# Linear attention with gates and a feed-forward layer: four masks of the first step go from VectorE to ScalarE and GpSimd, and the first step's matmuls are put in another order

## The chip, the cores and the metric

The kernel runs on one core of one Trainium2 chip. The metric is the device time of one execution in microseconds (us). The kernel before took 467.71, 467.12 and 467.70 us in three runs, a median of 467.7 us. A change of under 0.2% (0.94 us) is about what a measurement of this kernel cannot tell from no change.

## The reference, cut to what matters

Four batches, eight heads, 768 tokens, head size 48. A gated linear attention is followed by a feed-forward layer of 384 to 2048 to 384 with a piecewise activation:

```
f = 1 / (1 + exp(-f_logit))
for t in range(S):
    state = f[:, :, t, :, None] * state + einsum('bhd,bhde->...', k[:, :, t], v[:, :, t])
    y[:, :, t] = einsum('bhd,bhde->bhe', q[:, :, t], state)
x = y.transpose(0, 2, 1, 3).reshape(B * S, H * D)          # 3072 x 384
h = x @ w_in                                               # 384 -> 2048
g = where(h >= 1, h, where(h <= -1, 0, (h + 1) ** 2 / 4))
out = g @ w_out                                            # 2048 -> 384
```

## The kernel before, in words

**Tiles and stages.** The tokens are taken in six steps of 128 (C) for all four batches (B), so 512 columns (N) at a time. Within a step the recurrence is written as matrix products: scores (keys times queries, each scaled by running products of the gates), a mask that keeps the pairs with an earlier key, and the masked scores times the values. The feed-forward layer takes each step's 512 columns in 16 units of 128 hidden rows: nine 128x512 matmuls into `ph` (L317; unit 0 is written out at L960), the activation on ScalarE and VectorE (L320 to L334), and nine into `po` (L341). Its products are made of high and low halves, which is why there are nine. 96 units in all fill most of the time.

**The start.** Before unit 0 can begin, step 0's attention has to be ready. Its gates come in three tiles, 0 to 2; a fourth pair of heads rides in spare rows of the three ("last"). For each tile VectorE runs a scan into `w` (L546), a reciprocal (L552), a second scan (L553), and multiplies keys (L556) and queries (L558) in `kq`; tiles 0 and 2 are taken in two halves of 256 columns. TensorE then makes the scores of a tile (L638, into two PSUM banks), and the scores of the last pair (L668), whose keys ScalarE has copied to `kn` (L662). VectorE multiplies each bank by the 0/1 mask, which is a constant in `fixed` (L681, `masks`): `am` 0 to 3 for the banks of tiles 0 and 1, and `act`, `kn`, `am` 0 and 1 again for tile 2 and the last pair. TensorE multiplies the masked scores by the values: two groups "first" (L917, `heads`) that need the masks of tiles 0 and 1, then four groups "second" (L932, `thirds`, and L917) that need the others. The results are rounded to `x` (L761 on ScalarE, L762 on VectorE), and unit 0 starts.

**GpSimd** (POOL) has small work only: three instructions of 2 to 4 columns for each gate tile (L550, L563, L565).

**What sets the order.** Every operation is recorded with an engine, a cost in ns (`COST`) and what it needs. `Plan.order` plays them through by these costs and emits each engine's instructions in the order that comes out; `LOOK` names the engines that may pass over a ready operation for a more urgent one that is nearly ready. TensorE's operations keep the order in which they were recorded, which the tuple `START` gives for step 0. Where the plan foresees TensorE idle, it puts fillers in, matmuls on a tile of zeros into a bank that nobody reads (L396, `warm`); how many is worked out in `zeros_for`:

```
if o.start < 20000 and gap > 250:
    return int(gap / (330 if o.start < 10000 else 230)) + 1
return int(gap * 0.9 / 230) if gap > 500 else 0
```

A filler is emitted into TensorE's own stream and keeps its place there like any other matmul; what TensorE really waits for at run time does not change their number.

Of the kernel before, what the change touches and what calls it, by code (L numbers as in the profile page):

```python
# [19 lines left out]
ALU = mybir.AluOpType  # L20
PSUM = bass.MemoryType.PSUM

B, H, S, D = 4, 8, 768, 48
C = 128
# [28 lines left out]
LATENCY = dict(PE=235, ACT=140, DVE=110, POOL=150)  # L53
COST = dict(mm=227, narrow=120, scores=1000, scores_half=500, heads=960, thirds=1020, half=330, both=940, begin=430, before=880, part=450, states=700, before_half=440, parts=730, parts_last=730, zeros=4000, turn=395, first=160, last=200,
            rows=316, turned_rows=150, scan=1140, dve=602, small=200, sums=467, gate=600, act=575, bits=660, round=485, copy=520, turned=412, sig=538, decay=226,
            issue=480, near=600, least=300)


INSTRUCTIONS = dict(scores=32, scores_half=16, heads=32, thirds=32, both=128, begin=64, before=128, before_half=64, part=64, states=64, parts=128, parts_last=64, zeros=24, turn=8)
BLOCK, FIRST_BLOCK, AHEAD, BEHIND, FETCH, OFFSET, WAITS = 256, 193, 48, 40, 3700, 9, 1.0045  # L60


LOOK, MARGIN, GAP = ("ACT", "DVE"), 100, 3000

SOONER = 2000
GATHER_BEHIND, GATHER_LATER = (0, 0, 0), 6000
# [2 lines left out]
VISITS = {4: (8.0, 8.0, 11.0, 11.0), 6: (11.0, 12.5, 12.5, 12.5), 8: (21.0, 21.0, 22.0, 22.0), 10: (25.0, 25.0, 28.5, 28.5), 12: (28.5, 34, 36.0, 36.0), 14: (36.0, 42.5, 42.5, 42.5), 16: (49.0, 49.0, 55.0, 55.0), 18: (54.0, 55.0, 57.0, 57.0), 20: (66.0, 66.0, 75.0, 75.0), 22: (75.0, 77, 77, 77)}  # L69
HOMES = [(k + 3) % 5 for k in range(25)]  # L70
START = (("scores", 0), ("mask", 0, 0), ("mask", 0, 1), ("last", 0), ("scores", 1), ("mask", 1, 0), ("mask", 1, 1), ("last", 1),
         ("scores", 2, 0), ("last", 2, 0), ("scores", 2, 1), ("last", 2, 1), ("first", 0), ("first", 1),
         ("mask", 2, 1), ("mask", 3, 1), ("mask", 2, 0), ("mask", 3, 0), ("second", 0), ("second", 1), ("second", 2), ("second", 3))
AFTER = {1: (('turn', 0), ('turn', 1), ('turn', 2)), 4.5: (('states', 0), ('states', 2)), 2: (('turn', 3),)}

# [23 lines left out]
class Plan:  # L99
# [7 lines left out]
    def add(self, engine, cost, emit, *deps, kb=0, count=None):  # L107
        flat, made = [], count is not None

        def spread(d):  # L110
            if isinstance(d, list):
                for e in d:
                    spread(e)
            elif d is not None and d not in flat:
                flat.append(d)

        spread(list(deps))
        cost, kind = COST[cost] if isinstance(cost, str) else cost, cost
        count = count or INSTRUCTIONS.get(kind) or 2 * max(1, round(cost / (COST["mm"] if cost % COST["mm"] == 0 else COST["narrow"])))
        if engine == "PE":  # L120
            if self.tensor is not None and self.tensor not in flat:
                flat.append(self.tensor)
            small = made or kind in SMALL_PRODUCTS
            cost += (COST["last"] if small else COST["first"]) if small != self.small else 0
            self.small = small
        o = Op(engine, cost, emit, flat, kb)
        if engine == "PE":
            o.count = count
        for d in flat:
            d.users.append(o)  # L130
        if engine == "PE":
            self.tensor = o
        self.ops.append(o)
        return o
# [96 lines left out]
def gla_moe(ctx: ExitStack, tc: tile.TileContext, ff, kqd, f0, vv, vad, vbd, wd, fixedd, gates, values, headsd, out):  # L231
    nc = tc.nc
# [4 lines left out]
    def tiles(count, shape, dtype, name):  # L237
        return [const.tile(shape, dtype, name=f"{name}_{k}") for k in range(count)]
# [11 lines left out]
    am = tiles(4, [C, B, C], F32, "am")  # L250
# [28 lines left out]
    def wide(a):  # L279
        return a.rearrange("r b c -> r (b c)")  # L280

    def part(t, k):

        return t[:, k * N:(k + 1) * N].rearrange("r (b c) -> r b c", b=B)

    def whole(t):
        return t[:, 2 * N:]
# [63 lines left out]
    add = plan.add  # L351

    def dma(dst, src, kb, *deps):
        return add("SP", "issue", lambda: nc.sync.dma_start(dst, src), *deps, kb=kb)
# [4 lines left out]
    def vec(cost, fn, *deps):  # L359
        return add("DVE", cost, fn, *deps)  # L360

    def sca(cost, fn, *deps):
        return add("ACT", cost, fn, *deps)
# [130 lines left out]
    banks = {k: [] for k in range(8)}  # L494
# [11 lines left out]
    gates_of = [None] * (NI * NT)  # L506
# [3 lines left out]
    def old(n, *names, of=att):  # L510

        return [] if n < 0 else [of[n].get(k) for k in names]

    def gate(m):

        i, p = divmod(m, NT)
        t = kq[p]

        ft, before = (f[m], None) if m < 2 else (act_f[1], None) if m == 2 else (f[(m - 1) % 2], m - 3 if m < 5 else m - 2)
        et = end[m % 2]  # L520
        steps = ((0, 2), (2, 4)) if m in (0, 2) else ((0, 4),)
        count = len(steps)
        c = gates_of[m] = {k: [] for k in ("km", "qm", "sg", "en", "s1", "s2")}
        lk = c["lk"] = dma(t[:, 0:2 * N], kqd[i, p], 512, old(NP * (i - 1) + p, "sc", "y", "tr"),
                           old(m - NT, "km", "qm", "to", of=gates_of))
        if m == 0:
            ready["mask"] = ready["mask_t"] = ready["ident"] = dma(fixed, fixedd, 160)
            ready["f0"] = sca(200, lambda: nc.scalar.activation(f0s[:, 0:NI * NT * B], f0s[:, 0:NI * NT * B], AF.Sigmoid), dma(f0s, f0, 36))
        for h, (b0, b1) in enumerate(steps):
            cols = slice(b0 * C + (1 if b0 else 0), b1 * C + 1)  # L530
            if m != 2:
                l = dma(ft[:, cols], ff[i, p, :, cols], 256 // count, gates_of[before]["qm"] if before is not None else None)
            elif h == 0:
                l = dma(ft[:, 0:N + 1], ff[i, p, :, 0:N + 1], 256)
                l.early = SOONER
            last = old(m - 1, "km", "en", "s2", of=gates_of)
            u0, u1 = B - b1, B - b0
            fwd = ft[:, b0 * C:b1 * C]
            bwd = ft[:, b1 * C:b0 * C:-1]
            kt, qt = wide(part(t, 0)[:, u0:u1]), wide(part(t, 1)[:, b0:b1])  # L540
            if m != 2:
                sg = sca("sig" if count == 1 else 308, lambda cols=cols: nc.scalar.activation(ft[:, cols], ft[:, cols], AF.Sigmoid), l)  # L542
            elif h == 0:
                sg = sca("sig", lambda: nc.scalar.activation(ft[:, 0:N + 1], ft[:, 0:N + 1], AF.Sigmoid), l)

            s1 = vec(COST["scan"] if count == 1 else 602, lambda bwd=bwd, u0=u0, u1=u1: nc.vector.tensor_tensor_scan(  # L546
                out=wide(w[:, u0:u1]), data0=bwd, data1=wide(least_w[:, u0:u1]), initial=0.0,
                op0=ALU.mult, op1=ALU.max), sg, c["sg"], set_least, last)
            last_w = w[:, u1 - 1:(u0 - 1 if u0 else None):-1, C - 1]
            en = add("POOL", "least", lambda b0=b0, b1=b1, last_w=last_w: nc.gpsimd.tensor_copy(  # L550
                out=et[:, b0:b1], in_=last_w), s1, old(m - 2, "pf", of=gates_of))
            rc = vec("small", lambda b0=b0, b1=b1, last_w=last_w: nc.vector.reciprocal(out=rec[:, b0:b1, 0], in_=last_w), s1, last, set_rec)  # L552
            s2 = vec(COST["scan"] if count == 1 else 602, lambda fwd=fwd, b0=b0, b1=b1: nc.vector.tensor_tensor_scan(  # L553
                out=fwd, data0=fwd, data1=wide(rec[:, b0:b1]), initial=0.0, op0=ALU.mult, op1=ALU.add), rc, s1, c["s1"])
            c["s1"].append(s1)
            km = vec(COST["gate"] if count == 1 else 335, lambda kt=kt, u0=u0, u1=u1: nc.vector.tensor_tensor(  # L556
                out=kt, in0=kt, in1=wide(w[:, u0:u1]), op=ALU.mult), s1, lk)
            qm = vec(COST["gate"] if count == 1 else 335, lambda qt=qt, fwd=fwd: nc.vector.tensor_tensor(  # L558
                out=qt, in0=qt, in1=fwd, op=ALU.mult), s2, lk)
            for name, d in (("sg", sg), ("en", en), ("km", km), ("qm", qm), ("s2", s2)):  # L560
                c[name].append(d)
        to, f0m = whole(t), f0s[:, m * B:m * B + B]
        o = add("POOL", "least", lambda: nc.gpsimd.tensor_tensor(out=to, in0=et, in1=f0m, op=ALU.mult),  # L563
                c["en"], ready["f0"], c["lk"], old(NP * (i - 1) + p, "db"))
        c["pf"] = [o, add("POOL", "least", lambda: nc.gpsimd.tensor_copy(out=f0m, in_=to), o)]  # L565

    va = sd[:, 0:4 * B * 64].rearrange("u (b h e) -> u b h e", b=B, h=4)
    vb = v_all[:, 0:B * 384].rearrange("u (b e) -> u b e", b=B)
# [12 lines left out]
    def elementwise(n):  # L581
# [5 lines left out]
        for m in ours:  # L587
            if gates_of[m] is None:
                gate(m)
# [84 lines left out]
    def masks(n, h):  # L674

        c = att[n]
        c.setdefault("am", [None, None])
        b, ps, _ = c["held"][h]
        t = am_of[n][h]
        free = {(2, 0): lambda: att[0]["ys"][0], (3, 0): lambda: att[0]["ys"][1], (3, 1): lambda: att[3]["pt"][1]}.get((n, h), lambda: None)  # L680
        o = vec("dve", lambda: nc.vector.tensor_tensor(  # L681
            out=t, in0=ps, in1=mask.rearrange("u (o t) -> u o t", o=1).broadcast_to([C, B, C]), op=ALU.mult),
            c["sc"], ready["mask"], free())
        banks[b][:] = [o]
        c["am"][h] = o
# [493 lines left out]
    with tc.If(fits < 1, label="general"):  # L1179
# [7 lines left out]
        with tc.For_i(0, S, 1) as t:  # L1187
# [15 lines left out]
            for n in range(2):  # L1203
                ps = wide(pa[n])
# [7 lines left out]
        with tc.For_i(0, NI, 1) as i:  # L1212
# [3 lines left out]
            for kt in range(3):  # L1216
                ps = wide(pa[kt])
# [96 lines left out]
```

## Time and profile before

| what | value |
|---|---|
| median of three runs | 467.7 us |
| the profiled execution: span from first to last instruction | 465.4 us |
| the runs' median less that span | 2.3 us |
| granted TensorE clock, mean | 0.998 |
| first matmul of unit 0 (L960) | 23.18 us |
| TensorE busy | 460.2 us, 99% |
| VectorE busy | 368.9 us, 79% |
| ScalarE busy | 268.5 us, 58% |
| GpSimd busy | 25.3 us, 5% |

The profiled execution has its span on record, and the time around the span is taken as the 2.3 us by which the runs' median is above it. In the rows further down PE is TensorE, DVE VectorE, ACT ScalarE and POOL GpSimd; times count from the start of the span. A busy TensorE in the profile does not tell useful matmuls from fillers, and a duration in a row contains some overlap with the next instruction of the same engine, so distances between starts are read rather than durations where something is added up.

### The profile page before, as it was taken

Reading aid. Unit: us, or ns where it says so; the run is one execution under the profiler, and the core shown is the slowest. Engines: PE = TensorE matmul, PEld = TensorE weight load, DVE = VectorE, ACT = ScalarE, POOL = GpSimd, SP = SyncE. Lnnn points to the kernel's source line nnn. Section 1 sums busy time; section 2 is a strip of 40 time slices with the busy share of each in tenths; the row PEclk is TensorE's granted clock in tenths of the full one; section 3 lists DMA queues with packets and bytes.
Section 4 is the critical chain, followed back from the end, with each engine's and each line's share of the span. In section 5 each row is a group of like instructions: output and inputs, shape, how many; then the busy total and the mean of one; then the engine's idle time right before and its main releaser. Section 6 shows DMA issues by size and latency. Waiting matters only on the chain.

```text
span 465.4 us, 10974 instructions
## 1 busy us (share of the span) xinstructions
PE 460.2 (99%) x4551; PEld 378.2 (81%) x4551; DVE 368.9 (79%) x709; ACT 268.5 (58%) x502; POOL 25.3 (5%) x67
## 2 busy tenths in 40 slices
PE   9999999999999999999999999999999999999996
PEld 4888888888888888888888888888888888888885
DVE  7999998899999999888889987867665565655633
ACT  4599999765565646546547344556445544554443
POOL 4100110000002000002001000000000000000000
PEclk9999999999999999999999999999999999999999
DMA  8897855271050252031424016603402323434101
GB/s 293 324 330 279 296 177 170 78 216 51 3 159 1 54 130 85 28 116 48 127 56 125 25 47 200 174 2 75 142 1 86 98 78 94 159 104 123 45 0 72
DMA packets 20308, 54.35 MB, mean 117 GB/s; under 512 B 3328, under 2 KB 3968, under 8 KB 20256
## 3 DMA queue, kind: packets, MB, share of 16 engines
q1 hardware_dynamic: 20256, 53.63, 36.7%
q8 instruction: 36, 0.59, 0.5%
q14 instruction: 16, 0.13, 0.1%
HBM read 44.77 MB, written 4.72 MB: 106 GB/s over the span
## 4 chain that ended last, share of the span: by engine, by line
PE 99%; DVE 0%; ACT 0%; issue 0%; DVEq 0%
PE po L341 43%; PE ph L317 42%; PE pa L777 2%; PE ph L396 2%; PE pa L808 2%; PE ph L716 2%; PE pa L884 1%; PE pa L742 1%; PE ph L668 1%; PE ph L960 0%; PE pa L716 0%; PE pa L932 0%; PE pa L917 0%; PE po L638 0%; PE pa L863 0%; PE ph L884 0%
## 5 line engine op out<-in xcount | busy, mean ns | idle before, releaser
L317 PE MATMUL ph<-x,w_hi 128*128 128x512 f32 x570 | 145.4, 391 | 0.0
L320 ACT ACTIVATE act<-ph,half 128x512 f32<-128x512 f32 x96 | 66.0, 687 | 108.6 <-PE ph L317 108.3
L317 PEld LDWEIGHTS ph<-x,w_hi 128*128 128x128 f32 x570 | 106.6, 188 | 22.2
L328 DVE SCALAR_TENSOR_TENSOR act<-ph,act 128x512 f32<-128x512 f32 x96 | 66.1, 688 | 44.3 <-ACT act L323 43.2
L331 ACT CAST ghi<-act 128x512 fp32r<-128x512 f32 x96 | 59.5, 620 | 60.8 <-DVE act L328 60.4
L341 PE MATMUL po<-ghi,w_hi 128*128 128x512 f32 x287 | 84.3, 396 | 0.0
L341 PE MATMUL po<-ghi,w_lo 128*128 128x512 f32 x287 | 82.6, 390 | 0.0
L341 PE MATMUL po<-glo,w_hi 128*128 128x512 f32 x287 | 82.6, 390 | 0.0
L334 DVE TENSOR_TENSOR glo<-act,ghi 128x512 fp32r<-128x512 f32 x96 | 66.2, 689 | 18.5 <-ACT ghi L331 16.1
L317 PE MATMUL ph<-x,w_lo 128*128 128x512 f32 x285 | 80.1, 389 | 0.0
L756 DVE STREAM_TRANSPOSE kn<-kq 32x128 f32<-32x128 f32 x224 | 67.8, 303 | 3.6
L341 PEld LDWEIGHTS po<-ghi,w_lo 128*128 128x128 f32 x287 | 53.9, 188 | 11.4
L341 PEld LDWEIGHTS po<-glo,w_hi 128*128 128x128 f32 x287 | 53.9, 188 | 11.3
L317 PEld LDWEIGHTS ph<-x,w_lo 128*128 128x128 f32 x285 | 53.5, 188 | 11.2
L323 ACT ACTIVATE act<-act 128x512 f32<-128x512 f32 x96 | 60.7, 632 | 2.7
L341 PEld LDWEIGHTS po<-ghi,w_hi 128*128 128x128 f32 x287 | 52.7, 188 | 10.9
L469 DVE TENSOR_REDUCE ok<-raw 128x1 f32<-128x512 f32 x48 | 31.4, 680 | 13.6 <-DMA raw<-in_w 13.6
L550 POOL COPY end<-w 128x4 f32<-128x4 f32 (+1 forms) x20 | 7.1, 357 | 282.9 <-DVE w L546 242.9
L546 DVE TENSOR_TENSOR_SCAN w<-f,least_w 128x512 f32<-128x512 f32 (+1 forms) x18 | 20.7, 1157 | 2.0 <-ACT f L542 2.0
L553 DVE TENSOR_TENSOR_SCAN f<-f,rec 128x512 f32<-128x512 f32 (+1 forms) x18 | 20.7, 1156 | 0.1
L457 DVE TENSOR_TENSOR w_lo<-bits,w_hi 128x512 fp32r<-128x512 f32 (+1 forms) x25 | 16.1, 662 | 0.2
L456 ACT CAST w_hi<-bits 128x512 fp32r<-128x512 f32 (+1 forms) x25 | 14.5, 598 | 0.8 <-DVE bits L452 0.8
(138 smaller groups left out, 396.2 us busy)
## 6 DMA issues: line engine op xcount, KB each, us to landing
kq<-in_kq SPq DMA_DIRECT2D x18, 512.0 KB, 4.4
raw<-in_w SPq DMA_DIRECT2D x18, 512.0 KB, 3.6
raw<-in_w SPq DMA_DIRECT2D x14, 511.6 KB, 5.2
out_y<-raw SPq DMA_DIRECT2D x17, 256.0 KB, 2.5
f<-in_f SPq DMA_DIRECT2D x16, 256.5 KB, 2.9
v<-in_v SPq DMA_DIRECT2D x10, 384.0 KB, 4.6
raw_late<-in_w SPq DMA_DIRECT2D x7, 511.6 KB, 4.8
raw<-in_w SPq DMA_DIRECT2D x12, 256.0 KB, 3.8
```

Of the source, the lines that this page charges most:

```text
L317: nc.tensor.matmul(ps[:, to], w_in(w_hi if high else w_lo, j, kt), xt[:, kt, t, c], start=(n == 0), stop=(n == 8))
L320: nc.scalar.activation(a, ps, AF.Relu, bias=half, scale=0.5)
L323: nc.scalar.activation(a, a, AF.Square)
L328: nc.vector.scalar_tensor_tensor(out=a, in0=ps, scalar=1.0, in1=a, op0=ALU.max, op1=ALU.min)
L331: nc.scalar.copy(hi, a)
L334: nc.vector.tensor_tensor(out=lo, in0=a, in1=hi.bitcast(F32), op=ALU.subtract)
L341: nc.tensor.matmul(po[e][:, c], w_out(part, j, e), g[:, of], start=(j == 0 and n == 0 and c.start == 0), stop=(j == NJ - 1 and n == 2))
L457: l = vec(COST["dve"] * n // W, lambda: nc.vector.tensor_tensor(out=lo, in0=whole_val, in1=hi.bitcast(F32), op=ALU.subtract), h)
L469: seen.append(vec("dve", lambda z=z, op=op: nc.vector.tensor_reduce(out=ok[:, 1 + NG + z + c:2 + NG + z + c], in_=words_of(raw[2])[1].bitc ...
L546: s1 = vec(COST["scan"] if count == 1 else 602, lambda bwd=bwd, u0=u0, u1=u1: nc.vector.tensor_tensor_scan(out=wide(w[:, u0:u1]), data0=bw ...
L553: s2 = vec(COST["scan"] if count == 1 else 602, lambda fwd=fwd, b0=b0, b1=b1: nc.vector.tensor_tensor_scan(out=fwd, data0=fwd, data1=wide( ...
L756: nc.vector.transpose(kn[n % 2][u:u + 32, ::-1, r:r + 32], src[:, :, u:u + 32])
```

## The change

Four of the eight masks of step 0 (tiles 0 and 1, `n < 2`) are no longer made by VectorE. ScalarE copies the PSUM bank to `am`, and GpSimd sets to zero in place the elements that the mask would (`affine_select`). The bank is then free after the copy. The first scan of tile 1 (`m == 1`) now also waits for tile 0's queries, so these stand ahead of it on VectorE. `START` puts the group ("first", 0) between the halves of tile 2's scores. The planner's costs and its list `LOOK` change with it.

```
-            issue=480, near=600, least=300)
+            issue=480, near=600, least=400, pf=620, select=850)
-LOOK, MARGIN, GAP = ("ACT", "DVE"), 100, 3000
+LOOK, MARGIN, GAP = ("ACT", "DVE", "POOL"), 100, 3000
-         ("scores", 2, 0), ("last", 2, 0), ("scores", 2, 1), ("last", 2, 1), ("first", 0), ("first", 1),
+         ("scores", 2, 0), ("last", 2, 0), ("first", 0), ("scores", 2, 1), ("last", 2, 1), ("first", 1),
...
-            last = old(m - 1, "km", "en", "s2", of=gates_of)
+            last = old(m - 1, "km", "en", "s2", *["qm"] * (m == 1), of=gates_of)
...
-        o = add("POOL", "least", lambda: nc.gpsimd.tensor_tensor(out=to, in0=et, in1=f0m, op=ALU.mult),
+        o = add("POOL", "pf", lambda: nc.gpsimd.tensor_tensor(out=to, in0=et, in1=f0m, op=ALU.mult),
...
         free = {(2, 0): lambda: att[0]["ys"][0], ...
+        if n < 2:
+            o = sca("copy", lambda: nc.scalar.copy(wide(t), wide(ps)), c["sc"])
+            banks[b][:] = [o]
+            c["am"][h] = add("POOL", "select", lambda: nc.gpsimd.affine_select(
+                out=t, in_=t, pattern=[[0, B], [1, C]], compare_op=ALU.is_ge, fill=0.0, base=1 - C, channel_multiplier=1), o)
+            return
```

On TensorE, behind the scores of tile 0 (L638, `kq_0`) and ahead of the last pair's (L668), the filler (L396: a weight load of `zeros` and a matmul) stood twice. Before:

```order
L638 MATMUL pa0_112<-kq_0_68 128x128
L638 MATMUL pa1_113<-kq_0_68 128x128
L396 LDWEIGHTS zeros_63
L396 MATMUL ph1_116<-zeros_63 128x512
...
L668 MATMUL ph0_115<-kq_0_68,kn_0_80 128x128
L668 MATMUL po1_118<-kq_0_68,kn_0_80 128x128
```

The same place now, where the pair of L396 rows stands eight times:

```order
L638 MATMUL pa0_112<-kq_0_68 128x128
L638 MATMUL pa1_113<-kq_0_68 128x128
L396 LDWEIGHTS zeros_63
L396 MATMUL ph1_116<-zeros_63 128x512
...
L668 MATMUL ph0_115<-kq_0_68,kn_0_80 128x128
L668 MATMUL po1_118<-kq_0_68,kn_0_80 128x128
```

Six fillers have come in here. Ahead of tile 0's scores three have gone (27 before, 24 now), so TensorE has three more than before in all; its other rows are the same ones, with the group ("first", 0) moved as `START` says.

On GpSimd, in the stretch of the gate tiles 0 to 2, the four selections (`am_0` to `am_3`) come between the small instructions:

```order
 L563 TENSOR_TENSOR kq_0_68<-end_0_74,f0s_104 128x4
+L684 AFFINE_SELECT am_0_76<-am_0_76 128x512
+L565 COPY f0s_104<-kq_0_68 128x4
+L684 AFFINE_SELECT am_1_77<-am_1_77 128x512
+L550 COPY end_0_74<-w_73 128x2 x2
+L684 AFFINE_SELECT am_2_78<-am_2_78 128x512
+L684 AFFINE_SELECT am_3_79<-am_3_79 128x512
 L563 TENSOR_TENSOR kq_1_69<-end_1_75,f0s_104 128x4
-L565 COPY f0s_104<-kq_0_68 128x4
 L565 COPY f0s_104<-kq_1_69 128x4
-L550 COPY end_0_74<-w_73 128x2 x2
```

Tile 1's small product (`kq_1`) now stands behind all four.

On VectorE, from tile 2's second half of queries (`kq_70`, L558) on, the four masks are gone, and one conversion of weights (`bits_95`, L452) has moved ahead of the masks that are left (L687 is L681 of before):

```order
 L558 TENSOR_TENSOR kq_70<-kq_70,act_84 128x256
-L681 TENSOR_TENSOR am_76<-pa_112,fixed 128x512
-L681 TENSOR_TENSOR am_78<-po_117,fixed 128x512
-L681 TENSOR_TENSOR am_77<-pa_113,fixed 128x512
-L681 TENSOR_TENSOR am_79<-pa_114,fixed 128x512
-L681 TENSOR_TENSOR act_83<-ph_116,fixed 128x512
-L681 TENSOR_TENSOR kn_81<-po_118,fixed 128x512
 L452 SCALAR_TENSOR_TENSOR bits_95<-raw_late_102,bits_95 128x384
```

The masks into `act_83` and `kn_81` follow that conversion now. Earlier on VectorE tile 1's keys (L556, `kq_69`) have moved ahead of its second scan (L553). On ScalarE the copy into `am_0` stands ahead of the key copies (L662) of tiles 0 and 1, those into `am_1` and `am_2` behind them, and that into `am_3` between the two halves of tile 2's.

## Rows read from the trace of the kernel before

**Rows 1.** The page, its first line.

```profile
span 465.4 us, 10974 instructions
```

**Rows 2.** Waits of PE, whole span: waiter <- releaser: us, times, longest.

```profile
PE ph L396 <- DVE zeros L367: 1.1, 1, 1.1
```

**Rows 3.** Timeline of PE to 24 us: start, us, operation, out<-in, xcount.

```profile
1.08 8.33 PE L396 MATMUL ph<-zeros 128*128 128x512 bf16 x27 [1.08 <-DVE zeros L367]
9.34 1.16 PE L638 MATMUL pa<-kq 48*128 48x128 f32 x16
10.43 0.61 PE L396 MATMUL ph<-zeros 128*128 128x512 bf16 x2
...
13.85 1.04 PE L396 MATMUL ph<-zeros 128*128 128x512 bf16 x4
14.82 0.37 PE L638 MATMUL po<-kq 48*128 48x128 f32 x1
...
17.84 1.09 PE L917 MATMUL pa<-am,sd 128*64 128x128 f32 x16
18.86 0.41 PE L932 MATMUL po<-act,v 128*32 128x128 f32 x2
...
20.14 0.30 PE L932 MATMUL pa<-act,v 128*32 128x128 f32 x1
...
21.24 0.32 PE L932 MATMUL pa<-act,v 128*64 128x128 f32 x1
...
23.18 0.48 PE L960 MATMUL ph<-x,w_lo 128*128 128x512 f32 x1
```

**Rows 4.** Timeline of DVE, 7 to 19 us.

```profile
7.44 1.23 DVE L546 TENSOR_TENSOR_SCAN w<-f,least_w 128x512 f32<-128x512 f32 x1 [0.31 <-ACT f L542]
...
9.10 1.23 DVE L553 TENSOR_TENSOR_SCAN f<-f,rec 128x512 f32<-128x512 f32 x1
10.25 0.67 DVE L556 TENSOR_TENSOR kq<-kq,w 128x512 f32<-128x512 f32 x1
...
14.66 0.40 DVE L556 TENSOR_TENSOR kq<-kq,w 128x256 f32<-128x256 f32 x1
...
15.31 0.68 DVE L681 TENSOR_TENSOR am<-pa,fixed 128x512 f32<-128x512 f32 x1
...
18.30 0.68 DVE L681 TENSOR_TENSOR kn<-po,fixed 128x512 f32<-128x512 f32 x1
18.90 0.54 DVE L452 SCALAR_TENSOR_TENSOR bits<-raw_late,bits 128x384 uint32<-128x384 uint32 x1
```

**Rows 5.** DMA issues, 3.1 to 3.3 us: KB each, median us to landing.

```profile
kq<-in_kq SPq DMA_DIRECT2D x1, 512.0 KB, 5.8
```

**Rows 6.** Timeline of POOL: four small instructions, each by itself.

```profile
9.60 0.72 POOL L563 TENSOR_TENSOR kq<-end,f0s 128x4 f32<-128x4 f32 x1 [0.58 <-ACT f0s L528]
...
10.28 0.69 POOL L563 TENSOR_TENSOR kq<-end,f0s 128x4 f32<-128x4 f32 x1
...
30.44 0.20 POOL L563 TENSOR_TENSOR kq<-end,f0s 128x4 f32<-128x4 f32 x1
30.71 0.63 POOL L565 COPY f0s<-kq 128x4 f32<-128x4 f32 x1
```

**Rows 7.** Timeline of DVE, 30.0 to 31.1 us.

```profile
30.03 0.67 DVE L328 SCALAR_TENSOR_TENSOR act<-ph,act 128x512 f32<-128x512 f32 x1
30.61 0.68 DVE L457 TENSOR_TENSOR w_lo<-bits,w_hi 128x512 fp32r<-128x512 f32 x1
```

**Rows 8.** Groups of POOL by line and form: busy us, mean ns, idle before.

```profile
L379 POOL MEMSET kq<- 128x1028 f32 x1 | 1.0, 954 | 0.0
L372 POOL MEMSET rec<- 128x512 f32 x1 | 0.5, 524 | 0.4 <-POOLq L1305 0.4
```

**Rows 9.** Timeline of ACT, 15.1 to 16.2 us.

```profile
15.15 0.51 ACT L662 ACTIVATE kn<-kq,f0s 128x256 f32<-128x256 f32 x1 [0.67 <-DVE kq L556]
15.56 0.64 ACT L450 ACTIVATE bits<-raw_late,top_of 128x384 uint32<-128x384 fp8e4 x1
```

More of the change, by code (lines that the diff above doesn't have):

```diff
@@ L562, in gate @@
         to, f0m = whole(t), f0s[:, m * B:m * B + B]
-        o = add("POOL", "least", lambda: nc.gpsimd.tensor_tensor(out=to, in0=et, in1=f0m, op=ALU.mult),
+        o = add("POOL", "pf", lambda: nc.gpsimd.tensor_tensor(out=to, in0=et, in1=f0m, op=ALU.mult),
                 c["en"], ready["f0"], c["lk"], old(NP * (i - 1) + p, "db"))
-        c["pf"] = [o, add("POOL", "least", lambda: nc.gpsimd.tensor_copy(out=f0m, in_=to), o)]
+        c["pf"] = [o, add("POOL", "pf", lambda: nc.gpsimd.tensor_copy(out=f0m, in_=to), o)]
     va = sd[:, 0:4 * B * 64].rearrange("u (b h e) -> u b h e", b=B, h=4)
```

## The prediction

> **What bounds the kernel now.** I read four views in this order. The page gives the span of the profiled execution, 465.4 us [rows 1]; the runs' median of 467.7 lies 2.3 us above it, and I carry these 2.3 us over unchanged. The waits of TensorE say where it stood still: once, 1.1 us, at the very start [rows 2]. So from 1.08 us to the end it always had a matmul to run, and the time is the sum of what stands in its stream, fillers included. Its timeline up to 23.18 us shows that stream for the start: 27 fillers, tile 0's scores, 2 fillers, scores, 4 fillers, then the scores of tile 2, the heads, and unit 0 [rows 3]. VectorE's timeline shows a second chain that runs beside it almost without a gap (0.31 us at 7.44) [rows 4]. Its last mask that the second heads need, into `kn`, ends at 18.30 + 0.68 = 18.98, and the matmul group that waits for it starts at 18.86 on the half that is ready. That group takes 20.14 - 18.86 = 1.28 us, while the next one of the same form takes 21.24 - 20.14 = 1.10 [rows 3]: VectorE delays TensorE there by 0.18 us and nowhere else. TensorE and VectorE are nearly level, and whichever the change delays becomes the end of the start. Behind it nothing gives time back, as no later wait is there to absorb it [rows 2].
>
> **TensorE's own work.** Four fillers span 1.04 us and two 0.61 [rows 3], so one costs (1.04 - 0.61) / 2 = 0.215 us. Ahead of tile 0's scores three fall out: the scores start at 9.34 - 0.65 = 8.69, and their inputs are there, since the queries now stand ahead of a scan that itself starts at about 7.44 [rows 4]. Behind them six come in, 1.29 us. Net +0.65. The first heads between two halves of scores bring two more changes of kind. The fourth filler's end shows the price of one change: from 13.85 to 14.82 is 0.97 for four, 0.11 over 4 x 0.215 [rows 3]; two are 0.2. The 0.18 of the second heads can go. So TensorE alone gives 0.65 + 0.2 - 0.18 = +0.67 us, and it cannot give less than +0.47 (without the 0.2). Since TensorE had no other wait to lose, what VectorE is relieved of can earn no more than that 0.18, which is already taken off. With nothing else in the way, second heads would start at 18.86 + 0.67 + 0.18 = 19.7, near enough, and unit 0 at 23.85.
>
> **VectorE, without GpSimd.** Four masks go, whose pace is 0.60 us each (the first at 15.31; five of them reach to 18.30 - 15.31 = 2.99 us), 2.40 in all [rows 4]. The queries ahead of the scan fill the 0.31 us idle. But tile 1's keys have moved ahead of its second scan, and their data land 5.8 us after an issue at about 3.2, at 9.0 [rows 5]; before, that scan started at 9.10 and covered the landing. Now the keys start at about 9.05, take some 0.6 (their row's 0.67 overlaps the next), and the scan behind them 1.15 (9.10 to 10.25): tile 1's queries come at 10.8, where they stood before (10.25 + 0.6). Of the 0.31 us between nothing and 0.05 is left; I use 0.05. Tile 2's last keys end at 14.66 + 0.40 - 0.05 = 15.0 [rows 4].
>
> **GpSimd, the term that decides.** It has no row of a 512-column operation that reads. Its rows show something else: a 4-column product beside VectorE's scan from 9.10 takes 0.72 us and ends at 10.32, just as the scan gives way to the next multiplication at 10.25; the next one takes 0.69 and ends at 10.97, just behind that multiplication [rows 4, 6]. The same product takes 0.20 at 30.44, beside an instruction of VectorE that reads one operand from PSUM, and the copy at 30.71 takes 0.63 again beside one that reads two SBUF operands (0.68 from 30.61) [rows 6, 7]. So GpSimd stands while VectorE reads two SBUF tensors, and gets its turn at the end of that instruction. I take the reverse to hold as well: while a selection streams, a VectorE instruction with two SBUF operands stands. That half no row shows, because 4 columns are over too soon. VectorE works through such instructions without a break from 9.1 to 15.0, and all four selections fall in there: their copies come after tile 0's scores (about 9.9), behind two key copies (about 11.6), after tile 1's scores (about 13.8) and behind half a key copy (about 14.9). Each is worth P, the time for which it streams.
>
> Bounds of P: GpSimd's clearing of 512 columns takes 0.524 us and of 1028 columns 0.954 [rows 8], so a column costs (0.954 - 0.524) / 516 = 0.83 ns and 512 columns 0.43 us. That is the lower end, as a selection cannot write fewer. If reading and comparing go in turn with writing it is twice that, 0.85 us, the upper end. I take 0.6, the value between them by ratio. Below nothing it cannot be.
>
> [...]
>
> **The sum.** Tile 2's last keys end at 15.0 + 4P. From there the chain to the second heads: ScalarE starts its half of the key copy 0.09 behind them (15.06 to 15.15), the conversion L450 0.41 later, which ends after 0.64 [rows 9]; VectorE's L452, now ahead of the masks, takes 0.47 (the next start after 18.90 is a mask at 19.37; its row has 0.54 with overlap) [rows 4]; then a mask's pace of 0.60 and a mask's end of 0.68; with 0.05 for each of two hand-overs, 3.0 us. Second heads start at 18.0 + 4P, if that is later than 19.7; from there to unit 0 are 1.10 + (23.18 - 20.14) = 4.14 us [rows 3]. So unit 0 starts at 22.14 + 4P, which is 4P - 1.04 later than 23.18, and never less than 0.67 later. With P = 0.6: 24.54, +1.36 us. The copies on ScalarE (four of about 0.6) lie in its idle time, 0.67 us of it ahead of 15.15 alone [rows 9], and cost nothing; if that cover were gone, the chain above would start later by as much as it took. The small GpSimd products behind the selections feed nothing that step 0 needs. Behind the standing VectorE instructions are the last masks, the weight conversions and the roundings for unit 0, in nearly the order of before, so they are late by no more than the masks are. On SP the load of the mask constants has moved behind that of the values; the first mask was read at 15.31 and is read later now, which hides it. Span 465.4 + 1.36 = 466.8, time 469.1; I say 469.0.
>
> **Rivals.** (1) *Only the fillers count*: the selections stream for 0.43 us or less, or do not hold VectorE up. Then 4P - 1.04 is at most 0.68 and TensorE's own +0.67 decides: 468.4 us, no change that a measurement could tell. For it: tiny GpSimd instructions leave no delay on VectorE (10.25 follows 9.10 by a full-size scan's pace). Against it: two engines that shut each other out in one direction. Chance 0.34. (2) *Selections much dearer*, P of 1.0 and more, through slow code or a stop of TensorE so long that its clock falls: at P = 1.2, +3.8 and 471.5. For it: the small instructions' 0.2 us for 4 columns says GpSimd is not quick; against it the clearing at 0.83 ns a column. Chance 0.11. (3) *The other side, faster*: VectorE's relief reaches TensorE. It would decide if TensorE's rows hid waits, so that the chain through the `kn` mask, not the stream, set 18.86: that chain is shorter by four masks and longer by one conversion, 2.40 - 0.47 = 1.93 us, and with TensorE's own 0.67 the end comes 1.26 us earlier: 466.4. Against it: equal paces all along TensorE's rows and one wait in the whole span [rows 2, 3]. Chance 0.05. The forecast has 0.50.
>
> **How the numbers follow.** A change of under 0.2% (0.94 us) cannot be told from none in this kernel. The forecast covers P from 0.5 (where 4P - 1.04 passes 0.94) to 0.9: 468.6 to 470.3. Rival 1 reaches down to 467.9 with the +0.47 and the scatter of the runs, rival 2 up to 472. The range 467.8 to 470.9 leaves out rival 3 (0.05), the upper part of rival 2 (0.08) and a little at rival 1's lower edge. Slower 0.60 (forecast 0.50 and rival 2, less a part of the forecast near 0.94), same 0.35, faster 0.05.
>
> **What would show it.** Right: unit 0 (L960) starts near 24.5; VectorE's instructions between 10 and 16 us are stretched or spaced by about P at four places, each beside a selection; the selections last 0.6 to 1.2 us with their wait; TensorE now waits for VectorE at the second heads. The filler step: tile 0's scores at 8.7, the last pair's at 11.6. Wrong: VectorE's scans keep their pace of 0.60 and 1.15 beside a running selection (then rival 1), or unit 0 starts before 23.6 (then TensorE's stream was not what counted).

## The result, and the profile after

The changed kernel takes 472.56 us (median of four runs, 472.40 to 472.71) against 467.70 for the kernel before on the same chip: ratio 1.0103, 95% interval 1.0090 to 1.0116. It is slower, by 4.9 us, and 1.7 us beyond the upper end of the predicted range. The profiled span grew by 5.2 us, at a granted clock of 0.997 (0.998 before). The page's first line and its row for the queue that brings the engines' code, which had 36 packets before:

```profile
span 470.6 us, 10980 instructions
...
q8 instruction: 37, 0.61, 0.6%
```

TensorE's timeline of the start answers to [rows 3]:

```profile
1.15 8.02 PE L396 MATMUL ph<-zeros 128*128 128x512 bf16 x24 [1.15 <-DVE zeros L367]
9.10 1.16 PE L638 MATMUL pa<-kq 48*128 48x128 f32 x16
10.20 1.90 PE L396 MATMUL ph<-zeros 128*128 128x512 bf16 x8
12.03 0.37 PE L668 MATMUL ph<-kq,kn 64*128 64x128 f32 x1
...
14.91 1.04 PE L396 MATMUL ph<-zeros 128*128 128x512 bf16 x4
...
20.11 0.30 PE L938 MATMUL po<-act,v 128*32 128x128 f32 x1
...
24.26 0.48 PE L966 MATMUL ph<-x,w_lo 128*128 128x512 f32 x1
```

Unit 0 starts at 24.26, 1.08 us later than at 23.18. From the first scores on it is 24.26 - 9.10 = 15.16 us, where it was 23.18 - 9.34 = 13.84: +1.32, which is the six fillers at 0.215 (1.29) and a remainder of 0.03. The first scores gained only 0.24, not the 0.65 of three fillers fewer. TensorE waits nowhere in this stretch behind its first instruction.

VectorE's timeline of the same stretch answers to [rows 4], GpSimd's to [rows 6]:

```profile
9.14 0.69 DVE L556 TENSOR_TENSOR kq<-kq,w 128x512 f32<-128x512 f32 x1 [0.18 <-DMA kq<-in_kq]
...
11.04 1.10 DVE L558 TENSOR_TENSOR kq<-kq,f 128x512 f32<-128x512 f32 x1
...
13.29 0.73 DVE L556 TENSOR_TENSOR kq<-kq,w 128x256 f32<-128x256 f32 x1
13.94 0.68 DVE L553 TENSOR_TENSOR_SCAN act<-act,rec 128x256 f32<-128x256 f32 x1
...
15.00 1.12 DVE L553 TENSOR_TENSOR_SCAN act<-act,rec 128x256 f32<-128x256 f32 x1
16.04 0.78 DVE L556 TENSOR_TENSOR kq<-kq,w 128x256 f32<-128x256 f32 x1
...
17.95 0.56 DVE L452 SCALAR_TENSOR_TENSOR bits<-raw_late,bits 128x384 uint32<-128x384 uint32 x1 [0.79 <-ACT bits L450]
18.75 0.69 DVE L687 TENSOR_TENSOR act<-ph,fixed 128x512 f32<-128x512 f32 x1 [0.25 <-PE ph L638]
19.36 0.68 DVE L687 TENSOR_TENSOR kn<-po,fixed 128x512 f32<-128x512 f32 x1
```

```profile
10.95 0.64 POOL L684 TENSOR_SCALAR_AFFINE_SELECT am<-am 128x512 f32<-128x512 f32 x1 [1.03 <-ACT am L682]
...
12.66 1.09 POOL L684 TENSOR_SCALAR_AFFINE_SELECT am<-am 128x512 f32<-128x512 f32 x1 [0.48 <-ACT am L682]
...
14.77 1.78 POOL L684 TENSOR_SCALAR_AFFINE_SELECT am<-am 128x512 f32<-128x512 f32 x2 [0.17 <-ACT am L682]
```

Four instructions of VectorE are stretched, each beside one selection. A 512-column product takes 1.10 (0.69 undisturbed, the row at 9.14), the 256-column ones 0.73 and 0.78 (0.40 undisturbed, the second half's key product of [rows 4]), a 256-column scan 1.12 (0.68 at 13.94, the same scan of the other half). That is +0.41, +0.33, +0.38 and +0.44, a mean of 0.39. Yet the second heads do not wait for it: the mask into `kn` ends at 19.36 + 0.68 = 20.04, and TensorE comes to them at 20.11. VectorE even stands idle twice. The 0.79 us for ScalarE's conversion L450 belong to its own chain, as that conversion stands behind a key copy that had to wait for VectorE's keys (1.27 us, at 16.86). The 0.25 for TensorE's own scores do not: by them TensorE is the later of the two.

So the start explains 1.08 of 5.2 us. The second piece is far away. The waits of TensorE, of the whole execution:

```profile
PE ph L396 <- DVE zeros L367: 1.2, 1, 1.2
...
PE ph L814 <- ACT seen_y L794: 0.8, 1, 0.8
```

Of these, [rows 2] had only the first. The chain of waits around the second one (start, length, what):

```profile
289.87 4.00 DMA f<-in_f
293.87 0.02 issue
293.89 0.63 ACT f L542
294.53 0.58 ACT act L320
295.10 0.05 ACT seen_y L794
...
295.19 0.26 PE ph L814 x2
```

ScalarE waits for a load of gates, turns it into sigmoids (L542), and only then makes the small copy `seen_y` that TensorE waits for. In the kernel before, L542 stood behind that copy, and before L542 ScalarE had done four decays (L614) and an activation. Its rows there:

```profile
292.58 0.14 ACT L788 COPY seen_y<-ph 1x8 f32<-1x8 f32 x1
...
293.32 0.63 ACT L542 ACTIVATE f<-f 128x513 f32<-128x513 f32 x1
```

In the changed kernel, from the start of the matmul ahead of the wait to that of the one behind it is 0.97 us, nearly all of it lost (0.95); 0.1 more goes in a wait at 328.6, and as much in smaller steps. Together about +1.15.

The third piece is at the end. From the start of the last matmul to the end of the span it is 470.6 - 463.23 = 7.37 us, before 465.4 - 461.00 = 4.37. The instructions of the line that tests the result (L1185, before L1179) show it; columns are the engine's sequencer, the operation, its length in ns (least/median/most) and its start in us. After:

```profile
L1185 PEldq COMPARE_BRANCH  x1: 4102/4102/4102, 465.4 to 465.4; - x1
```

And before:

```profile
L1179 PEldq COMPARE_BRANCH  x1: 388/388/388, 463.2 to 463.2; - x1
```

TensorE's last branch takes 4.10 us in place of 0.39. The other engines' branches take under 0.1 in both. SyncE, which closes the program, then waits for TensorE:

```profile
SPq L1314 <- PEq L1185: 3.0, 1, 3.0
```

The pieces are 1.08 + 1.15 + 3.0 = 5.2 us. Two of the three lie far from the work that the change was meant for.

### The profile page after: what moved, and what is told of

It reads as the page before. It is cut to its first block, busy times and chain, and to the rows that moved or that the text cites. A ratio compares the mean times of both kernels' runs of the same rounds, so it can differ in the third digit from the quotient of the medians.

```text
span 470.6 us, 10980 instructions
## 1 busy us (share of the span) xinstructions
PE 461.6 (98%) x4554; PEld 378.3 (80%) x4554; DVE 368.3 (78%) x705; ACT 270.4 (57%) x506; POOL 27.3 (6%) x71
## 4 chain that ended last, share of the span: by engine, by line
PE 96%; DVE 1%; DMA 1%; ACT 0%; issue 0%; DVEq 0%
PE po L341 41%; PE ph L317 41%; PE ph L396 2%; PE pa L783 2%; PE ph L722 2%; PE pa L814 2%; PE pa L890 1%; DMA f<-in_f 1%; PE pa L748 1%; PE ph L668 1%; PE ph L966 0%; PE pa L722 0%; PE po L638 0%; PE pa L938 0%; PE pa L923 0%; PE pa L869 0%
## 5 line engine op out<-in xcount | busy, mean ns | idle before, releaser
L553 DVE TENSOR_TENSOR_SCAN f<-f,rec 128x512 f32<-128x512 f32 (+1 forms) x18 | 20.8, 1158 | 0.0
```

## The experiments

Theory: the time goes (i) in the fillers that the planner's costs put into TensorE's stream, which are there at the start and also shift a border between pieces of code to TensorE's closing branch; (ii) in ScalarE's new order near 290 us, which the costs `least` and `pf` make; (iii) the selections do hold VectorE up, but beside TensorE's longer stream it does not show in the time. Rival: the masks' new path itself costs the time, and end and wait follow from it.

**Five fillers in place of eight.** The changed kernel with the fillers behind the first scores cut, so that TensorE's stream is as long as before:

```
-                warm(o.zeros)
+                warm(o.zeros - 3 * (o.zeros == 8))
```

> The changed kernel with five fillers instead of eight behind tile 0's scores; nothing else is moved, and TensorE's stream is then as long as before the change. Theory (the 3.0 us at the end are TensorE's branch, 4.10 us instead of 0.39, waiting for code because three fillers more put the branch's target into a piece of code that is not there yet): the branch falls back to about 0.4 us, unit 0 starts 0.65 us sooner (23.6), total 472.6 - 3.0 - 0.65 = 468.9 us. Rival (the long branch comes from the added code on GpSimd and ScalarE, or from the later end as such): only the 0.65 us go, 471.9 us, and the branch stays near 4 us.

469.23 us, ratio to before 1.0035 (1.0022 to 1.0049): 3.3 us less than the changed kernel. The branch takes 0.40 us again, unit 0 starts at 23.50. The chain at 290 us is still there, and in this profile longer (1.82 us between starts):

```profile
289.35 4.59 DMA f<-in_f
293.94 0.02 issue
293.96 0.63 ACT f L542
```

Three fillers, worth 0.65 us by their own length, carry 3.3.

**The costs of GpSimd's small work as before.** The changed kernel with `least` at 300 and the product's cost `pf` at 300; this moves only ScalarE's L542 and L614 and rows of GpSimd.

```
-            issue=480, near=600, least=400, pf=620, select=850)
+            issue=480, near=600, least=300, pf=300, select=850)
```

> The changed kernel with the planner's costs of GpSimd's small work set back (least=300, pf=300); the only rows that move are on ScalarE near 290 us (the gates' sigmoid back behind the state's decay) and on GpSimd. Theory (the 0.8 us wait of TensorE at 295 us is the sigmoid standing in ScalarE's queue in front of what TensorE needs, waiting for its load to land): the wait goes, and with it 0.95 to 1.15 us: 471.4 to 471.6 us. Rival (the load itself comes later because everything is 1 us late, so something waits there anyway): no gain, 472.5 us.

471.71 us, ratio 1.0082 (1.0065 to 1.0099), 0.85 less than the changed kernel and a little less of a gain than expected. The interval overlaps that of the changed kernel (1.0090 to 1.0116), so this run alone does not prove the gain. There is no wait at 295 us, and the branch is as long as ever:

```profile
L1185 PEldq COMPARE_BRANCH  x1: 4127/4127/4127, 464.7 to 464.7; - x1
```

**Both edits together.**

> Both edits: five fillers and the costs set back. If the three causes add up, 472.6 - 3.65 - 1.1 = 467.8 us, within 0.3 us of the kernel before: the masks' move then costs and gains nothing by itself. If VectorE, held up by the selections, is the end of the start, unit 0 cannot follow the fillers and the time stays over 468.4 us.

467.84 us, ratio 1.0011 (1.0001 to 1.0021). The two edits give back 3.33 + 0.85 = 4.2 alone and 4.7 together, so they are nearly additive. With five fillers on both sides the costs are worth 469.23 - 467.84 = 1.39 us, and there the intervals lie apart (1.0022 to 1.0049 and 1.0001 to 1.0021). What is left, the masks' new path and order, is 0.2 us slower than before, less than the 0.94 us that a measurement can tell; so the rival falls. No kernel that was run beats the one before. With five fillers TensorE does wait for what VectorE and ScalarE prepare:

```profile
PE ph L668 <- ACT kn L662: 0.3, 1, 0.3
PE po L638 <- DVE kq L558: 0.3, 1, 0.3
```

**Three fillers more in the kernel before.** None of the masks moved, only TensorE's stream is as long as in the changed kernel.

```
-                warm(o.zeros)
+                warm(o.zeros + 3 * (o.zeros == 2))
```

> The kernel before with three fillers more behind tile 0's scores (five instead of two) and no other edit. Theory: 0.65 us at the start and the long branch at the end, 467.7 + 0.65 + 3.0 = 471.3 us. Rival (the end has nothing to do with the length of TensorE's stream): 468.3 us with a branch of about 0.4 us.

469.70 us, ratio 1.0032 (1.0016 to 1.0047), ten runs in two lots: four from 468.1 to 468.7, six from 469.4 to 470.9. The profile is of the longest run and has the branch:

```profile
L1179 PEldq COMPARE_BRANCH  x1: 4087/4087/4087, 464.0 to 464.0; - x1
```

So fillers alone make the long branch; the masks are not needed for it. None of the shorter lot was profiled, but 468.12 less the 3.0 us of the branch would be 465.1, while the kernel before, with less work, never took under 466.9: in these four runs the branch must have been shorter. The same program can then have it or not. The median came out between theory and rival.

**One filler more, and six more, in the kernel before** (`+ 1` and `+ 6` in the same line). The question is whether the branch grows with the stream or meets a border.

> The kernel before with one filler more (three instead of two). If the long branch at the end starts at a certain length of TensorE's stream, between 0 and 3 fillers more, this tells on which side one lies: 467.6 + 0.2 = 467.8 us with a branch of 0.4 us, or 470.8 us with one of 4 us. The two modes of e4 (468.1 to 468.7 and 469.4 to 470.9 us) make me expect the short one.

467.73 us, ratio 1.0001 (0.9986 to 1.0015), branch 0.39.

> The kernel before with six fillers more (eight instead of two), as many behind tile 0's scores as in the changed kernel. Theory (length of the stream alone): 467.6 + 1.29 + 3.0 = 471.9 us with a branch of about 4 us in every run. If the branch is long only near a border of the stream's length, 468.9 us with a short one.

468.47 us, ratio 1.0017 (1.0004 to 1.0029). The branch is short, so length alone falls as a cause:

```profile
L1179 PEldq COMPARE_BRANCH  x1: 487/487/487, 464.8 to 464.8; - x1
```

**Three fillers more in the changed kernel**, 11 behind the first scores: it does more work, and its stream is as long as the one just shown.

> The changed kernel with three fillers more, 11 in place of 8 behind the first scores, so that TensorE's stream is as long as in the kernel before with six fillers more. Theory (the 4 us at TensorE's last branch come from where the border of a piece of code lies, not from the changed work): the branch is short again, under 0.6 us in place of 4.10, the piece is fetched before the branch is reached; unit 0 starts 0.6 to 1.3 us later than 24.26, and the time is 470.2 to 470.9, so less than the changed kernel's 472.56 although it does more. Rival (the branch is long by what the change does, or grows with the stream): it stays at 4 us, and the time is 473.2 to 473.9.

470.06 us, just under the range expected, ratio 1.0059 (1.0046 to 1.0072): 2.5 us less than the changed kernel, for 0.65 us more of work. The branch is 0.49 us:

```profile
L1185 PEldq COMPARE_BRANCH  x1: 487/487/487, 464.6 to 464.6; - x1
```

The step on unit 0 missed: it starts at 24.02, not later than 24.26, since the first fillers ran faster in this profile (below). The profiled run was the shortest of six (468.43; the others 469.6 to 470.9), so whether each of the others had a short branch is not known; all six lie more than 1.5 us below the shortest run of the changed kernel (472.40).

What goes with the branch's length is when a piece of code is fetched. The changed kernel's code queue, asked for the two single microseconds in which it moved something near the end, 466 to 467 and 470 to 471:

```profile
q8 instruction: 1, 0.02, 10.4%
...
q8 instruction: 1, 0.02, 8.3%
```

The branch starts at 465.4; a fetch follows within 1.1 us, the branch ends at 469.55, and the next fetch comes 0.7 later. With three fillers more (the run just shown), from 460 to 461, 3.7 us ahead of the branch at 464.6:

```profile
q8 instruction: 1, 0.02, 5.8%
```

The profiles fall in three kinds by the instructions in the page's first line. With 10974 or 10976 (before, five fillers, both edits, one more, and both kernels with other selections, of which one counts four more on GpSimd) there is one fetch at the end, behind a short branch. With 10980 (the changed kernel, the same with the costs as before, and the kernel before with three more) there are two, the first behind the branch's start, and the branch is long in all three. With 10986 (six more; the changed kernel with three more) one lies ahead of the branch and one behind it, and it is short. The pieces are of 16 KB (0.61 MB in the changed kernel's 37, 16384 bytes each), and the branch takes 3.7 us more (4.10 against 0.39) where the first of two fetches starts behind the branch's start. That the branch waits for this very piece is the author's reading of the times: in the three profiles with a long branch it ends 1.36 to 1.42 us behind the end of that fetch (466.48 + 1.67 = 468.15 in the changed kernel, and the branch ends at 469.55), although the fetch starts 1.01 to 1.55 us behind the branch's start. No run moved the branch's target alone, so that a border decides is not shown, and it would not be all, as the shorter lot of the kernel before with three more shows.

**Selections of 4 columns**, on the kernel with both edits; of the masks of tiles 0 and 1 only these columns are applied.

> The kernel of e3 with each selection cut to 4 of its 512 columns, so that the masks of tiles 0 and 1 are not applied; copies, waits and order stay. Theory (a selection that streams holds up VectorE's instructions with two SBUF operands): the stretched ones, tile 1's queries (1.09 us), tile 2's first keys (0.73), its second keys (0.79) and queries (0.85), fall back to 0.68, 0.40, 0.40 and 0.42 us; tile 2's last queries end 1.5 us sooner (at about 15.7), and unit 0 starts at 23.1 instead of 23.58, bound by TensorE's stream. Rival (ScalarE's copies into the same tiles or TensorE stretch them): the rows stay as they are.

467.98 us in one run, too little to compare. VectorE's rows:

```profile
10.77 0.69 DVE L558 TENSOR_TENSOR kq<-kq,f 128x512 f32<-128x512 f32 x1
...
12.62 0.41 DVE L556 TENSOR_TENSOR kq<-kq,w 128x256 f32<-128x256 f32 x1
...
14.61 0.40 DVE L556 TENSOR_TENSOR kq<-kq,w 128x256 f32<-128x256 f32 x1
14.92 0.42 DVE L558 TENSOR_TENSOR kq<-kq,act 128x256 f32<-128x256 f32 x1
```

Every stretch is gone. Tile 2's queries end at 15.34 in place of 16.37 + 0.85 = 17.22 with full selections, which is 1.88 sooner. Of this 1.54 are the four stretches of the full selections (0.40, 0.32, 0.39 and 0.43 us), and 0.34 is an earlier landing: VectorE starts tile 1's keys at 8.88 and not, after a wait for their load, at 9.22. Unit 0 starts at 22.85 in place of 23.58. The columns streamed are what holds VectorE.

**Each selection twice**, on the same kernel.

> The kernel of e3 with each selection done twice, the second on the result of the first. Theory: each second one holds VectorE for another 0.35 to 0.45 us wherever it works on two SBUF operands; tile 2's last queries end 1.2 to 1.8 us later than 17.2, and unit 0 starts 1.0 to 1.8 us later than 23.58. Rival (VectorE only yields once, at the first): no change beyond 0.2 us.

469.4 us in one run; unit 0 at 24.85, +1.27, as expected, but not by the way expected. Tile 2's last queries end only 0.56 later (17.78), where 1.2 to 1.8 was expected; tile 1's keys started 0.43 sooner (8.79), so the second selections added 0.99. The +1.27 comes from two waits of TensorE ahead of the second half of tile 2's scores, which start at 18.58 in place of 17.31: one for VectorE's queries of the first half, and one for GpSimd itself.

```profile
PE po L638 <- DVE kq L558: 0.7, 1, 0.7
PE po L926 <- POOL am L686: 0.3, 1, 0.3
```

GpSimd's last four selections take 3.50 us in a row:

```profile
15.72 3.50 POOL L686 TENSOR_SCALAR_AFFINE_SELECT am<-am 128x512 f32<-128x512 f32 x4
```

They run past VectorE's last two-operand product (16.93 + 0.85), so a part of them no longer holds VectorE up. A doubled cost need not double its effect when it runs out of the stretch in which it collides.

## Why the prediction was wrong

**Slower** was right, and so was TensorE's stream as the floor: from the first scores to unit 0, +1.32 measured against six fillers' 1.29, with 0.2 for two changes of kind and 0.18 gained (1.31).

**The selections hold VectorE up**: right as a mechanism, in the direction that no row of before showed, and shown by the 4-column run. P was mis-sized: 0.39 us against the 0.6 taken, and below the lower bound of 0.43, which came from clearing memory. So 4P - 1.04 is 0.52 and not 1.36; it lies under TensorE's own floor of 0.67. "Unit 0 = 22.14 + 4P" was not what decided. At the start rival 1 held: only the fillers count, and VectorE's idle 0.25 shows that it was no longer the later of the two. It is again with five fillers, where TensorE waits, and there the formula holds: 22.14 + 4 x 0.39 = 23.70, and unit 0 starts at 23.50 and 23.58.

**Tile 0's scores at 8.69**: they came at 9.10, as 13 of the first fillers ran at the long pace and not 11. Without these 0.41 us the start would have cost 0.67 to 0.83, an estimate: 0.67 by TensorE alone, and 1.08 less the 0.25 that VectorE had to spare. With the same fillers ahead of the scores it was 8.21 in the run with three more behind them, so this term is chance, and no property of the change; what goes with it is the clock (last section).

**The landing of tile 1's keys** held: VectorE waited 0.18 us at 9.14 for them. What the queries fill was lost again, and more: tile 1's queries start at 11.04, 0.2 later than before.

**The step that failed** is "Behind it nothing gives time back, as no later wait is there", read as: behind the start nothing changes, and the end and the 2.3 us around the span are the same. (Around the span it is 472.40 - 470.6 = 1.8 us, as in nearly all runs on record; about 0.5 of the 2.3 was that the profiled execution of before was shorter than the median.) The view of TensorE's waits says that no wait exists to be saved; it does not say that none can be made. Both later pieces were made by parts of the change that the prediction priced only at the start (the fillers) or not at all (the costs). The costs `least` and `pf` apply to every gate tile, and in the one near 290 us they put L542, which waits for a load, ahead of the copy that TensorE needs: 0.85 us between medians with eight fillers, 1.39 with five. And three fillers more in TensorE's stream were counted as 0.65 us, without the 3 us that six more instructions cost at the closing branch. Rival 2, the only case that came near in time (471.5), was wrong in its mechanism.

Not all of the wait at 295 us is the order's. It stands in all three profiles with the changed order (0.97, 1.82 and, with three fillers more, 0.49 us between starts), but also in two of eight with the order of before (0.84 and 0.76). In one of these, the kernel before with one filler more, VectorE waited for another load:

```profile
288.96 0.69 DVE L556 TENSOR_TENSOR kq<-kq,w 128x512 f32<-128x512 f32 x1 [1.01 <-DMA kq<-in_kq]
```

The stretch has little to spare, and a late landing alone can open the wait. The new order makes it depend on one more load: in the kernel before with three fillers more that load landed later than in any profile with the new order (295.13 against 293.94 at most), and TensorE did not wait for the copy. What it costs over many runs, the medians show and the profiles do not.

## What to carry to other kernels

Read a change of costs or of fillers over the whole program, not at the place it was meant for: compare each engine's order to the end, and ask of every instruction that moved ahead whether it waits for a load and who stands behind it. When a stream gets some instructions longer or shorter, look at the closing branch in the trace before looking for a reason in the work; a few instructions more can be cheaper than a few less, as here (470.06 us with 11 fillers behind the first scores, 472.56 with 8). And an engine without waits is a bound for what can be saved, not a promise that nothing can be lost.

## What the runs showed of the hardware

- TensorE's closing branch takes 0.39 to 0.49 us or 4.09 to 4.13, and as far as the fetches' times show, by when a 16 KB piece of code is fetched: long in the three profiles with 6 instructions more than before, where the first fetch near the end starts 1.01 to 1.55 us behind the branch's start; short with 2 and with 12 more.
- While a selection of 512 columns streams on GpSimd, VectorE's instruction with two SBUF operands stands for 0.33 to 0.44 us in the changed kernel's profile. The selection's own row is 0.64 us at its shortest (10.95), and 1.09 at 12.66, beside scans that keep their pace (1.26 for two, as before); that it waits for VectorE in turn there is read from these rows.
- The same filler takes about 0.43 us at first and 0.215 later, a ratio of two like that of the two granted clocks the trace has on record, 1.00 and 0.50. The record at 0.50 lies at the end, where TensorE has stopped: before, it starts at 463.21 us, 1.9 behind the end of the last matmul (461.28), and in the changed kernel at 467.39, 3.9 behind it (463.51). The first record, at 1.00, starts at 6.59 us in the changed kernel and at 5.82 before, and the pace changes there: the fillers start 0.43 us apart up to 6.25 (before, 5.75) and 0.22 apart from 6.63 (6.01) on. Ahead of this record the trace has none, and a view prints 1.00 there too; that the clock is 0.50 at the long pace is therefore read from the pace and from this coincidence. The changed kernel's stretches of two us (x7 and x11 are TensorE's matmuls, the third number from the end the clock):

```profile
5.00:7.00 2.00, 2.00 (x7) 0.77 (x6) 2.00 (x6) 0.60 (x1) 0.17 (x1) 1.00 1.09 303
7.00:9.00 2.00, 2.00 (x11) 0.78 (x8) 1.93 (x4) 0.67 (x2) 0.19 (x1) 1.00 0.93 342
```

The engine was idle until 1.15 us and ran fillers without a gap from there. The number at the long pace was between 7, where the first scores began at 7.79 us behind 24 fillers (selections of 4 columns), and 14, where they began at 9.94 behind 27 (the kernel before with six more). What sets it was not tried.
